# A squared-ReLU feed-forward kernel: loading all x tiles first on two queues, transposing them in one block, and moving the small loads off GpSimd

## Chip, cores, metric

One core of one Trainium2 chip. The metric is the device time of one execution in microseconds (us). The profiled execution is one of those timed, except for the kernel before, where a further one of 291.46 us was profiled. "Span" is the profiled length from first to last instruction, about 1.7 to 2.1 us shorter than the device time.

## The reference

```python
B, S, D, F = 1, 2048, 576, 4608          # all bf16
def reference(x, w1, b1, w2, b2):
    h = jnp.einsum("bsd,df->bsf", x, w1) + b1
    r = jnp.where(h > 0, h, 0)
    h = r * r
    return jnp.einsum("bsf,fd->bsd", h, w2) + b2
```

## The kernel before

The sequence is cut into four blocks of 512 rows. D = 576 is four chunks of 128 rows and one half chunk of 64. The kernel treats 4 of the 36 column tiles of w1 (`w1n`, four 128-row chunks, and `w1n8`, the last 64 rows) apart from the rest (`w_h`). For the first block, x arrives as four row tiles, TensorE transposes them, VectorE and ScalarE copy the result out of PSUM, and the first four column tiles are computed from it chunk by chunk. That is the start-up stage, about the first 10 us, and it is nearly all that the change touches. After it come the half-row matmuls on `w_h` (PSUM tile `ph`) and the rest. The profile leaves numbers out of names: its `w_h` is `w1_h` in the code, `b_rows` is `b1_rows`, `x_sb` is `xs`, and `w1n` stands for both `w1n` and `w1n8`.

```python
    WARM = [512] * 6 + [128]
    for i, n in enumerate(WARM):                       # warm-up matmuls on a constant
        keep(nc.tensor.matmul(wps[:, 0:n], lhsT=ones[:, 0:P], rhs=ones[:, 0:n], start=True, stop=True))
    # ...
    load_x(nc.sync, 0)                                 # first loads: six from sync, two from ScalarE
    load_x(nc.scalar, 1)
    load_w1n(nc.sync, 0)
    load_x(nc.scalar, 2)
    load_w1n(nc.sync, 1)
    load_x(nc.sync, 3)
    for k in range(2, NK):                             # NK = 4
        load_w1n(nc.sync, k)
    # ... identity for the transposes on GpSimd
    nc.gpsimd.memset(b1_rows[:], 0.0)
    nc.gpsimd.dma_start(out=b1_rows[0:NFT, :], in_=b1.rearrange("(ft p) -> ft p", p=P))
    # ...
                # first block ("k_outer"): part(h, k) is 4 matmuls of 256 columns,
                # half h of the rows, chunk k
                for j in range(2):
                    for k in range(NK):
                        x_transpose(j, k)
                for j in range(2):
                    x_transpose(j, NK)
                x_copies(0)                            # chunks 0, 2: VectorE; 1, 3: ScalarE
                part(0, 0)
                for k in range(NK + 1):
                    x_transpose(2, k)
                part(0, 1)
                part(0, 2)
                for k in range(NK + 1):
                    x_transpose(3, k)
                x_copies(1)
                dup_windows(0)
                part(0, 3)
                part(1, 0)
                make_b1T()                             # transposes the bias rows, needed by the evictions
                for k in range(1, NK):
                    part(1, k)
    # ... then the half-row pairs on w1n8, then a_rows(0) on w_h
```

## Time and profile before

| | before |
|---|---|
| device time, 6 runs | 291.0 us median (290.65 to 291.53) |
| span of the profiled run | 289.6 us |
| PE busy | 285.5 us, 99% |
| first half-row `w_h` matmul | 10.29 us |

The page names the engine that bounds the kernel (part 1) and follows the chain of work that ended last (part 4). Columns of part 1: busy us, share of the span, number of instructions.

```profile
PE 285.5 (99%) x2027; PEld 139.9 (48%) x2032; DVE 78.6 (27%) x176; ACT 96.7 (33%) x154; POOL 2.3 (1%) x10
...
PE 98%; DMA 1%; issue 0%; DVE 0%
```

There is hardly idle time to win. The chain, read for the first microseconds alone, shows what can be moved (columns: start us, us, what):

```profile
...
0.73 2.99 DMA x_sb<-in_x_dram
3.73 0.04 issue
3.77 1.25 PE tb L149 x10
5.02 0.86 PE pn L227 x4
5.88 0.53 PE tb L149 x5
6.42 0.98 PE pn L227 x8
7.40 0.28 PE tb L149 x5
7.68 0.87 PE pn L227 x8
8.55 0.06 PE b1T_ps L166
8.61 1.31 PE pn L227 x12
...
```

After the first x tile there is no entry but PE, save 0.04 us of issue. The same work does not always cost the same: five transposes take 0.53 us at 5.88 and 0.28 us at 7.40. The array runs at half rate first and at full rate from about 6.5 us on. The page's row of granted clock does not show this (it has 9 in every slice), so it is read from the spacing of matmul starts: 107 then 56 ns for a transpose, 213 then 109 ns for 256 columns. The kept trace also holds a record of the granted clock; its full rate begins at 6.51 us here.

The busy time by stretches of the stage (columns: stretch, its length, then busy us and count for PE, weight loads, VectorE, ScalarE, GpSimd, then clock, DMA share, GB/s):

```profile
5.40:6.40 1.00, 1.00 (x9) 0.83 (x8) 0.15 (x1) 0.00 (x0) 0.18 (x1) 1.00 0.99 277
6.40:7.40 1.00, 1.00 (x12) 0.89 (x10) 0.00 (x0) 0.00 (x0) 0.00 (x0) 1.00 0.97 217
7.40:8.40 1.00, 1.00 (x14) 0.91 (x12) 0.80 (x4) 0.65 (x2) 0.00 (x0) 1.00 0.56 128
8.40:9.40 1.00, 1.00 (x12) 0.91 (x10) 0.97 (x2) 0.00 (x0) 0.00 (x0) 1.00 0.75 171
```

PE is busy in all of each. The bias rows, loaded from GpSimd, landed at 5.45 us and were wanted at 8.39: nobody waited for them.

### The profile page before, as it was taken

What the parts mean: (1) busy time and instruction counts of PE and PEld (TensorE: products, weight loads), DVE (VectorE), ACT (ScalarE), POOL (GpSimd) and SP (SyncE); (2) the same over time, 40 slices, a digit from 0 to 9 for tenths busy, and PEclk for the clock granted to TensorE, in tenths of its full rate; (3) what the DMA queues carried; (4) which work ended last, traced back from release to release, by engine and by line L of the source; (5) the groups of instructions that cost most, each with busy time, mean ns of one, the idle gap of its engine ahead of it and who ended that gap; (6) DMA issues with size and microseconds to landing.
All of it is one profiled execution on the core that took longest, in us unless ns stands there. A gap on an engine that the chain in (4) does not pass through costs nothing.

```text
span 289.6 us, 4693 instructions
## 1 busy us (share of the span) xinstructions
PE 285.5 (99%) x2027; PEld 139.9 (48%) x2032; DVE 78.6 (27%) x176; ACT 96.7 (33%) x154; POOL 2.3 (1%) x10
## 2 busy tenths in 40 slices
PE   8999999999999999999999999999999999999996
PEld 5544444444444555555544444444444455555555
DVE  1644554444500200000015444444440001100001
ACT  2566666666500000000027666666670000000000
POOL 3000000000000000000000000000000000000000
PEclk9999999999999999999999999999999999999999
DMA  7999999400001200000000000000000110000000
GB/s 198 221 245 188 308 389 212 92 0 2 0 14 25 52 16 18 16 16 18 16 16 2 1 2 0 2 0 2 0 2 0 36 38 16 16 16 19 33 16 18
DMA packets 31605, 16.52 MB, mean 57 GB/s; under 512 B 15700, under 2 KB 31584, under 8 KB 31584
## 3 DMA queue, kind: packets, MB, share of 16 engines
q1 hardware_dynamic: 31232, 15.91, 22.3%
q10 hardware_dynamic: 288, 0.30, 0.4%
q8 instruction: 16, 0.26, 0.4%
q14 instruction: 5, 0.04, 0.0%
q0 software_dynamic: 64, 0.01, 0.0%
HBM read 11.36 MB, written 2.36 MB: 47 GB/s over the span
## 4 chain that ended last, share of the span: by engine, by line
PE 98%; DMA 1%; issue 0%; DVE 0%
PE ph L188 42%; PE po L289 38%; PE pt L270 11%; PE pn L209 4%; PE pn L227 1%; DMA x_sb<-in_x_dram 1%; PE tb L149 1%; PE ph L190 1%; PE pn L203 1%; DVE o_sb L291 0%; PE b1T_ps L166 0%; PE pn L205 0%
## 5 line engine op out<-in xcount | busy, mean ns | idle before, releaser
L190 PE MATMUL ph<-xTw,w_h 64*128 64x512 bf16 x576 | 124.6, 376 | 0.0
L188 PE MATMUL ph<-xTw,w_h 64*128 64x512 bf16 x576 | 124.6, 376 | 0.0
L289 PE MATMUL po<-w_sb,hT 128*128 128x448 bf16 (+2 forms) x612 | 109.4, 341 | 0.0
L176 ACT ACTIVATE r<-ph,b1T 128x512 bf16<-128x512 f32 x128 | 81.1, 685 | 41.6 <-PE ph L190 41.6
L188 PEld LDWEIGHTS <-w_h 64*128 64x128 bf16 x576 | 54.1, 94 | 68.3
L289 PEld LDWEIGHTS <-hT 128*128 128x128 bf16 x612 | 58.5, 98 | 51.0
L177 DVE TENSOR_TENSOR hT<-r 128x512 bf16<-128x512 bf16 x144 | 61.2, 426 | 75.9 <-ACT r L176 75.5
L190 PEld LDWEIGHTS <-w_h 64*128 64x128 bf16 x576 | 54.1, 94 | 0.0
L291 DVE TENSOR_TENSOR o_sb<-po,b_bc 128x448 bf16<-128x448 f32 (+2 forms) x17 | 10.2, 597 | 125.8 <-PE po L289 125.8
L270 PE MATMUL pt<-hT,w_sb 128*128 128x512 bf16 x142 | 31.3, 379 | 0.1
L176 ACT ACTIVATE r<-pn,b1T 128x512 bf16<-128x512 f32 x16 | 10.3, 688 | 61.0 <-PE pn L205 59.6
L270 PEld LDWEIGHTS <-w_sb 128*128 128x128 bf16 x144 | 14.1, 98 | 17.0
L273 ACT ACTIVATE oT<-pt,b2T 128x512 bf16<-128x512 f32 x4 | 2.8, 688 | 28.3 <-PE pt L270 28.3
L209 PE MATMUL pn<-xTw,w1n 128*128 128x512 bf16 x45 | 10.4, 379 | 0.4 <-issue 0.3
L209 PEld LDWEIGHTS <-w1n 128*128 128x128 bf16 x48 | 4.5, 98 | 6.0 <-issue 0.8
L227 PE MATMUL pn<-xTw,w1n 128*128 128x256 bf16 x32 | 4.6, 295 | 0.0
L63 PE MATMUL wps<-const-bfloat16-1.0 128*128 128x512 bf16 (+1 forms) x7 | 2.8, 582 | 0.8 <-PEq L344 0.8
L227 PEld LDWEIGHTS <-w1n 128*128 128x128 bf16 x32 | 3.3, 107 | 0.5
L156 DVE COPY xTw<-tb 128x256 bf16<-128x256 bf16 x4 | 1.1, 292 | 6.7 <-PE tb L149 6.7
L119 DVE COPY xTw<-xTw 64x2048 bf16<-64x2048 bf16 x4 | 2.8, 690 | 0.2
L120 DVE COPY xTw<-xTw 64x2048 bf16<-64x2048 bf16 x4 | 2.7, 687 | 0.1
L149 PE MATMUL tb<-ident,x_sb 128*128 128x128 bf16 x20 | 2.4, 288 | 0.2 <-DMA x_sb<-in_x_dram 0.2
(23 smaller groups left out, 15.2 us busy)
## 6 DMA issues: line engine op xcount, KB each, us to landing
w_sb<-in_w_dram SPq DMA_DIRECT2D x4, 1296.0 KB, 12.7
w_h<-in_w_dram SPq DMA_DIRECT2D x14, 288.0 KB, 6.2
out_dram<-o_sb SPq DMA_DIRECT2D x15, 112.0 KB, 1.7
w_h<-in_w_dram SPq DMA_DIRECT2D x4, 144.0 KB, 3.5
w1n<-in_w_dram SPq DMA_DIRECT2D x4, 128.0 KB, 3.9
out_dram<-ot SPq DMA_DIRECT2D x4, 128.0 KB, 2.0
x_sb<-in_x_dram ACTq DMA_DIRECT2D x2, 144.0 KB, 2.9
x_sb<-in_x_dram SPq DMA_DIRECT2D x2, 144.0 KB, 3.4
```

Source lines behind the costliest of these rows:

```text
L63: keep(nc.tensor.matmul(wps[:, 0:n], lhsT=ones[:, 0:P], rhs=ones[:, 0:n], start=True, stop=True))
L149: keep(nc.tensor.transpose(bank[:, slot, qc], xs[:, j, c0:c0 + P], ident[:]))
L176: keep(nc.scalar.activation(out=r[:], in_=bank[:], func=ACT.Relu, bias=b1T[:, ft:ft + 1], scale=1.0))
L177: keep(nc.vector.tensor_tensor(out=hTs[sb][:, ft, :], in0=r[:], in1=r[:], op=ALU.mult))
L188: keep(nc.tensor.matmul(bx[:], lhsT=w1_h[0:H, LO_C[i], jc], rhs=xT[0:H, LO_W[i], :], start=(i == 0), stop=(i == NC - 1)))
L190: keep(nc.tensor.matmul(by[:], lhsT=w1_h[H:P, UP_C[i], jc], rhs=xT[H:P, UP_W[i], :], start=(i == 0), stop=(i == NC - 1)))
L203: keep(nc.tensor.matmul(banks[2 * i][:], lhsT=w1n8[0:H, i, :], rhs=xT[0:H, SPC, :], start=start, stop=stop, skip_group_check=order == "k_o ...
L209: keep(nc.tensor.matmul(banks[g][:], lhsT=w1n[:, k, g * P:(g + 1) * P], rhs=xT[:, O + k, :], start=start, stop=stop))
L227: keep(nc.tensor.matmul(banks[g][:, hc], lhsT=w1n[:, k, g * P:(g + 1) * P], rhs=xT[:, O + k, hc], start=(h == 0 and k == 0), stop=False, s ...
L270: keep(nc.tensor.matmul(pt[:], lhsT=w2_sb[:, ft, DM:D], rhs=hT[:, ft, :], start=(i == 0), stop=(i == NFT - 1)))
L289: keep(nc.tensor.matmul(po[:, 0:d1 - d0], lhsT=hT[:, ft, jj * P:(jj + 1) * P], rhs=w2_sb[:, ft, d0:d1], start=(i == 0), stop=(i == NFT - 1)))
L291: keep(nc.vector.tensor_tensor(out=o_sb[:, d0:d1], in0=po[:, 0:d1 - d0], in1=b2_bc[:, d0:d1], op=ALU.add))
```

## The change

Intent: let all x tiles arrive first, on two queues, and then the w1 chunks; transpose all of x before the first matmul; bring the last 64 rows of w1 in pieces of 1 KB instead of 256 bytes (each of the two loads then brings 64 KB instead of 32); take the loads off GpSimd; bring w2 in two loads instead of four. The number of TensorE instructions stays (the counts below differ by a few records that are missing from the traces). The core of the diff:

```diff
-    WARM = [512] * 6 + [128]
+    WARM = [512] * 6 + [256]
...
+    b1_rows = const.tile([P, P], BF16, name="b1_rows")
+    nc.vector.memset(b1_rows[:], 0.0)
     load_x(nc.sync, 0)
     load_x(nc.scalar, 1)
-    load_w1n(nc.sync, 0)
-    load_x(nc.scalar, 2)
-    load_w1n(nc.sync, 1)
-    load_x(nc.sync, 3)
-    for k in range(2, NK):
-        load_w1n(nc.sync, k)
+    load_x(nc.sync, 2)
+    load_x(nc.scalar, 3)
+    for k in range(NK):
+        load_w1n(nc.sync if k % 2 == 0 else nc.scalar, k, k + 1)
...
-    nc.gpsimd.memset(b1_rows[:], 0.0)
-    nc.gpsimd.dma_start(out=b1_rows[0:NFT, :], in_=b1.rearrange("(ft p) -> ft p", p=P))
...
     keep(nc.scalar.activation(out=warm[:], ...))      # its table load took 1.28 us
+    for h in range(2):
+        load_w1n8(nc.scalar, h)
+    keep(nc.scalar.dma_start(out=b1_rows[0:NFT, :], in_=b1.rearrange("(ft p) -> ft p", p=P)))
...
     def x_copies(h):
-        # chunks 0, 2 on VectorE; 1, 3 on ScalarE, one instruction each
+        for k in (0, 1):
+            keep(nc.vector.tensor_copy(out=xT0[:, O + k, hc], in_=tb[h][0][:, k, :]))
+        keep(nc.scalar.copy(out=xT0[:, O + 2:O + 4, hc], in_=tb[h][1][:, 0:2, :]))
...
                 for j in range(2):
-                    for k in range(NK):
-                        x_transpose(j, k)
-                # ... interleaved with part(0, 0) to part(0, 2)
+                    x_transpose(j)
                 x_copies(0)
+                for j in range(2, RT):
+                    x_transpose(j)
                 x_copies(1)
                 dup_windows(0)
-                part(0, 3)
+                for k in range(NK):
+                    part(0, k)
                 part(1, 0)
                 make_b1T()
                 for k in range(1, NK):
```

Left out: the PSUM pools of the transposes, the layout of `w1n8`, w2 in two loads, and the b2 column on the sync queue.

More of the change, by code (lines that the diff above doesn't have):

```diff
@@ L57 @@
     ps_o = ctx.enter_context(tc.tile_pool(name="ps_o", bufs=4, space=PSUM))
-    wps = ps_o.tile([P, 512], FP32, name="wps", tag="po")
+    wps = ps_h.tile([P, 512], FP32, name="wps", tag="ph")
     ones = nc.const_aps.tensor(1.0, [P, 512], BF16)
-    WARM = [512] * 6 + [128]
+    WARM = [512] * 6 + [256]
     for i, n in enumerate(WARM):
@@ L66 @@
     w1n = wpool.tile([P, NK, GW], BF16, name="w1n")
-    w1n8 = wpool.tile([P, G // 2, P], BF16, name="w1n8")
+    w1n8 = wpool.tile([P, GW], BF16, name="w1n8")
     w1_h = wpool.tile([P, NC, FH], BF16, name="w1_h")
@@ L72, in load_x, with load_w1n @@
         keep(eng.dma_start(out=xs[:, rt, :], in_=x2[rt * P:(rt + 1) * P, :]))
-    def load_w1n(eng, k):
-        keep(eng.dma_start(out=w1n[:, k, :], in_=w1[k * P:(k + 1) * P, 0:GW]))
+    def load_w1n(eng, k0, k1):
+        src = w1[k0 * P:k1 * P, 0:GW].rearrange("(k p) f -> p k f", p=P)
+        keep(eng.dma_start(out=w1n[:, k0:k1, :], in_=src))
     def load_w1n8(eng, h):
-        src = w1[NK * P:D, 0:GW].rearrange("p (i h f) -> p i h f", h=2, f=P)
-        keep(eng.dma_start(out=w1n8[h * H:(h + 1) * H, :, :], in_=src[:, :, h, :]))
+        keep(eng.dma_start(out=w1n8[h * H:(h + 1) * H, :], in_=w1[NK * P:D, 0:GW]))
     def load_w1(eng, h, j0, j1):
@@ L83, in load_w1 @@
                       in_=w1_v[:, :, GW + h * FH + j0 * P:GW + h * FH + j1 * P]))
+    b1_rows = const.tile([P, P], BF16, name="b1_rows")
+    nc.vector.memset(b1_rows[:], 0.0)
     load_x(nc.sync, 0)
     load_x(nc.scalar, 1)
-    load_w1n(nc.sync, 0)
-    load_x(nc.scalar, 2)
-    load_w1n(nc.sync, 1)
-    load_x(nc.sync, 3)
-    for k in range(2, NK):
-        load_w1n(nc.sync, k)
+    load_x(nc.sync, 2)
+    load_x(nc.scalar, 3)
+    for k in range(NK):
+        load_w1n(nc.sync if k % 2 == 0 else nc.scalar, k, k + 1)
     ident = const.tile([P, P], BF16, name="ident")
     make_identity(nc, ident[:])
-    b1_rows = const.tile([P, P], BF16, name="b1_rows")
-    nc.gpsimd.memset(b1_rows[:], 0.0)
-    nc.gpsimd.dma_start(out=b1_rows[0:NFT, :], in_=b1.rearrange("(ft p) -> ft p", p=P))
-    b2_col = const.tile([P, 1], BF16, name="b2_col")
-    nc.gpsimd.dma_start(out=b2_col[:], in_=b2[DM:D].rearrange("(d o) -> d o", o=1))
-    b2T = const.tile([P, 1], FP32, name="b2T")
-    nc.gpsimd.tensor_copy(out=b2T[:], in_=b2_col[:])
     warm = const.tile([P, 1], FP32, name="warm")
     keep(nc.scalar.activation(out=warm[:], in_=nc.const_aps.tensor(0.0, [P, 1], FP32), func=ACT.Relu))
+    for h in range(2):
+        load_w1n8(nc.scalar, h)
+    keep(nc.scalar.dma_start(out=b1_rows[0:NFT, :], in_=b1.rearrange("(ft p) -> ft p", p=P)))
     E3, O, SPC, E = 0, 1, 5, 6
@@ L130 @@
     w2_view = w2.rearrange("(ft p) d -> p ft d", p=P)
-    W2CH = 9
+    W2CH = 18
     def load_w2(c):
@@ L140, with x_transpose @@
     HS = SB // 2
-    tb_po = [ps_o.tile([P, 2, HS], BF16, name="tb", tag="po") for _ in range(2)]
-    tb_ph = [ps_h.tile([P, 2, HS], BF16, name="tb", tag="ph") for _ in range(4)]
-    half_banks = [tb_ph, None]
-    def x_transpose(j, k):
+    tb = [[ps_h.tile([P, 4, HS], BF16, name="tb", tag="ph") for _ in range(2)] for _ in range(2)]
+    PLACE = [(0, 0), (0, 1), (1, 0), (1, 1), (0, 2)]
+    T_ORDER = [0, 1, NK, 2, 3]
+    def x_transpose(j):
         h, q = divmod(j, 2)
-        qc = slice(q * P, (q + 1) * P)
-        bank, slot, c0 = (half_banks[h][k], 0, k * P) if k < NK else (half_banks[h][2], 1, D - P)
-        keep(nc.tensor.transpose(bank[:, slot, qc], xs[:, j, c0:c0 + P], ident[:]))
+        for k in T_ORDER:
+            bank, slot = PLACE[k]
+            c0 = k * P if k < NK else D - P
+            keep(nc.tensor.transpose(tb[h][bank][:, slot, q * P:(q + 1) * P], xs[:, j, c0:c0 + P], ident[:]))
     def x_copies(h):
         hc = slice(h * HS, (h + 1) * HS)
-        for k in range(NK):
-            src = half_banks[h][k][:, 0, :]
-            if k % 2 == 0:
-                keep(nc.vector.tensor_copy(out=xT0[:, O + k, hc], in_=src))
-            else:
-                keep(nc.scalar.copy(out=xT0[:, O + k, hc], in_=src))
-        keep(nc.vector.tensor_copy(out=xT0[:, E3, hc], in_=half_banks[h][2][:, 1, :]))
+        for k in (0, 1):
+            keep(nc.vector.tensor_copy(out=xT0[:, O + k, hc], in_=tb[h][0][:, k, :]))
+        keep(nc.scalar.copy(out=xT0[:, O + 2:O + 4, hc], in_=tb[h][1][:, 0:2, :]))
+        keep(nc.vector.tensor_copy(out=xT0[:, E3, hc], in_=tb[h][0][:, 2, :]))
     b1T = const.tile([P, NFT], FP32, name="b1T")
     def make_b1T():
-        b1T_ps = ps_o.tile([P, P], BF16, name="b1T_ps", tag="po")
+        b1T_ps = ps_h.tile([P, P], BF16, name="b1T_ps", tag="ph")
         keep(nc.tensor.transpose(b1T_ps[:], b1_rows[:], ident[:]))
@@ L198, in a_full @@
         for g in range(G):
-            pool, tag = (ps_o, "po") if g < 2 else (ps_h, "ph")
+            pool, tag = (ps_o, "po") if g < 2 or order == "k_outer" else (ps_h, "ph")
             banks.append(pool.tile([P, SB], FP32, name="pn", tag=tag))
         def pair(i, start, stop):
-            keep(nc.tensor.matmul(banks[2 * i][:], lhsT=w1n8[0:H, i, :], rhs=xT[0:H, SPC, :],
+            keep(nc.tensor.matmul(banks[2 * i][:], lhsT=w1n8[0:H, 2 * i * P:(2 * i + 1) * P], rhs=xT[0:H, SPC, :],
                              start=start, stop=stop, skip_group_check=order == "k_outer"))
-            keep(nc.tensor.matmul(banks[2 * i + 1][:], lhsT=w1n8[H:P, i, :], rhs=xT[H:P, E3, :],
+            keep(nc.tensor.matmul(banks[2 * i + 1][:], lhsT=w1n8[H:P, (2 * i + 1) * P:(2 * i + 2) * P], rhs=xT[H:P, E3, :],
                              start=start, stop=stop, skip_group_check=order == "k_outer"))
@@ L220, in a_full @@
             if order == "k_outer":
-                tb_new = [ps_h.tile([P, 2, HS], BF16, name="tb", tag="ph") for _ in range(2)]
-                half_banks[1] = tb_new + tb_po
                 def part(h, k):
@@ L231, in a_full @@
                 for j in range(2):
-                    for k in range(NK):
-                        x_transpose(j, k)
-                for j in range(2):
-                    x_transpose(j, NK)
+                    x_transpose(j)
                 x_copies(0)
-                part(0, 0)
-                for k in range(NK + 1):
-                    x_transpose(2, k)
-                part(0, 1)
-                part(0, 2)
-                for k in range(NK + 1):
-                    x_transpose(3, k)
+                for j in range(2, RT):
+                    x_transpose(j)
                 x_copies(1)
                 dup_windows(0)
-                part(0, 3)
+                for k in range(NK):
+                    part(0, k)
                 part(1, 0)
@@ L296 @@
         load_w1(nc.sync, 1, j0, j1)
-        if j0 == 0:
-            load_w1n8(nc.sync, 0)
-            load_w1n8(nc.sync, 1)
     load_xT(1)
@@ L303 @@
         load_w1(nc.sync, 1, j0, j1)
+    b2_col = const.tile([P, 1], BF16, name="b2_col")
+    keep(nc.sync.dma_start(out=b2_col[:], in_=b2[DM:D].rearrange("(d o) -> d o", o=1)))
+    b2T = const.tile([P, 1], FP32, name="b2T")
+    nc.gpsimd.tensor_copy(out=b2T[:], in_=b2_col[:])
     keep(nc.sync.dma_start(out=b2_bc[:], in_=b2.partition_broadcast(P)))
-    for c in (0, 2, 1, 3):
+    for c in range(2):
         load_w2(c)
```

## The prediction

> **What bounds it now.** TensorE. The page gives PE 285.5 us busy of a 289.6 us span (99%), and the chain that ended last is 98% PE. What is not PE on that chain is the first x tile's load (2.99 us, 1%) and the last eviction and store (286.9 us to the end). The waits of PE sum to 1.3 us. Everything the change touches, except the second half of the w2 loads, lies in the first 10.3 us, before the first half-row matmul of w1 (10.29 us in the timeline); w2 lands by 47.9 us and is first read at 76 us, so its two larger chunks, like the moved b2 loads, cost and gain nothing.
>
> **What PE does in those 10.3 us.** Warm-up from 0.78, then 20 transposes, 32 matmuls of 256 columns, the bias transpose and four half-row matmuls, from 3.77 us (first x tile landed at 3.73) with hardly a hole. I find two: 0.06 us before the first 256-column matmul, and 0.10 us before the half-row pairs (9.75 to 9.85), just after the second window copy on VectorE ended at 9.72. The rest of the lost time is the array's rate: starts are 107 ns apart for a transpose and 213 ns for 256 columns until about 6.5 us, then 56 and 109 ns. [...]
>
> **What the change does.** The instruction order shows the same number of TensorE instructions; only their order in this stage differs. All 20 transposes come first (20 x 107 = 2.14 us, to 5.91), then 32 matmuls, about 2.5 of them at half rate (estimate, if full rate comes again at 6.45): 5.91 + 0.54 + 29.5 x 0.109 + 0.056 = 9.72, half-row matmuls of w1 from about 10.15 instead of 10.29. So it saves the two holes, about 0.15 us. x tile 0 and 1 are first on their queues in both, so the 3.73 us stays. x tiles 2 and 3 should land near 4.2 to 4.6 instead of 4.1 and 6.1; the w1 chunks by about 6.3 instead of 7.05, none of which PE waited for. VectorE's window copies should end near 8.2 instead of 9.72.
>
> New risks: ScalarE now issues four loads (about 0.45 us each), a 1.28 us table load, then three more loads, so its first copy is near 5.5 us and the bias rows land near 7.8 to 8.2, wanted by PE near 8.35: slack of a few tenths. [...]
>
> **Prediction.** 290.6 us; 8 times in 10 between 289.9 and 291.5. The moment of full rate varies between runs (before: 290.65, 290.72, 291.53), more than the gain. Faster by over 2%: 0.005; within 2%: 0.99; slower by over 2%: 0.005.
>
> **What would show it.** Transposes in one block from about 3.77 to 5.9; no PE wait over 0.2 us; the first half-row w1 matmul at 10.0 to 10.3, if full rate comes near 6.4; from there to the end the same 279 us within 0.3.
>
> **What would make it wrong.** A late bias row or w1 chunk that stalls PE; [...] a later first x tile; a late w1 stream starving the half-row stage.

290.72, less the two holes of about 0.15 us, is about 290.6.

## The result, and the profile after

The changed kernel took 291.95 us (median of 6, 291.35 to 292.32) against 291.0 us. Ratios here and below are the mean time of a kernel's fast runs over that of the other kernel's fast runs of the same rounds, so they are not quite the ratio of the medians. This one is 1.0031, 95% interval 1.0016 to 1.0046: a loss of about 0.9 us, small but clear of the noise. The predicted 290.6 and its upper end 291.5 were both too low.

The same views of the changed kernel, parts 1 and 4 of the page first:

```profile
PE 285.9 (99%) x2032; PEld 139.8 (48%) x2032; DVE 78.4 (27%) x177; ACT 96.3 (33%) x152; POOL 0.9 (0%) x7
...
PE 98%; DMA 1%; DVE 0%; issue 0%
```

At this size of difference the averages say nothing. The chain of the first microseconds does:

```profile
...
0.78 2.93 PE wps L63 x7
3.71 1.93 PE tb L146 x18
5.63 3.04 DMA b_rows<-in_b_dram
8.67 0.05 issue
8.72 0.23 PE b1T_ps L159
8.95 1.31 PE pn L217 x12
...
```

The path that decides no longer runs through TensorE's matmuls in the middle of the stage. It runs through the load of the bias rows, issued at 5.63 us and landed at 8.67, and only 12 of the 32 matmuls remain on the chain after it. (The link from the transposes to the issue of this load is an inference of the view; what held the issue is shown below.) The stretches show what that leaves of PE:

```profile
5.40:6.40 1.00, 1.00 (x13) 0.92 (x11) 0.69 (x3) 0.16 (x1) 0.00 (x0) 1.00 0.64 164
6.40:7.40 1.00, 0.78 (x8) 0.56 (x6) 0.05 (x1) 0.92 (x2) 0.00 (x0) 1.00 1.08 252
7.40:8.40 1.00, 0.95 (x9) 0.60 (x7) 0.97 (x2) 0.00 (x0) 0.00 (x0) 1.00 1.00 227
8.40:9.40 1.00, 0.68 (x7) 0.63 (x8) 0.55 (x2) 0.00 (x0) 0.00 (x0) 1.00 0.88 216
```

There are two holes. Busy time hides a part of each, because the last matmul's modelled end runs into it; from start to start the first is 488 ns where 109 is normal (6.39 to 6.88 us), so 0.38 us, and the second 640 ns (8.08 to 8.72), so 0.53 us. Together 0.91 us. That this equals the loss of the medians is in part chance: the two profiles differ by only 0.34 us at the end of the stage, as the one of before was of one of its longer runs (291.46 us), with a late full rate. What the holes cost on average, the experiments have to show. The timeline names what ended them (columns: start, us, engine, line, operation, tiles, count, idle before and releaser):

```profile
3.93 0.20 ACT L97 ACTIVATE warm<-const-float32-0.0 128x1 f32<-128x1 f32 x1
4.12 0.49 ACTq L79 DMA_DIRECT2D w1n<-in_w_dram  x1
...
5.63 0.57 ACTq L100 DMA_DIRECT2D b_rows<-in_b_dram  x1
...
6.24 1.07 ACT L152 COPY xTw<-tb 128x512 bf16<-128x512 bf16 x2 [2.11 <-DVE xTw L151]
6.88 1.47 PE L217 MATMUL pn<-xTw,w1n 128*128 128x256 bf16 x12 [0.22 <-ACT xTw L152]
...
8.72 0.23 PE L159 MATMUL b1T_ps<-ident,b_rows 128*128 128x128 bf16 x1 [0.37 <-DMA b_rows<-in_b_dram]
```

ScalarE finished issuing the second small w1 load at 4.61 us. Its next instruction, the load of the bias rows, started at 5.63, a whole microsecond later, and the copy that stands behind it at 6.24, though its data (the transposes of x tiles 0 and 1) were in PSUM by 4.77. PE's first hole ends with that copy, the second with the bias rows. The releaser printed for the copy, VectorE, is the event that came last among its semaphores, not the reason: the queue itself was held.

What held it is a wait just ahead of the issue, which ended at 5.57 us. The view of this source line has it as an instruction of its own (count, duration in ns, first and last start in us):

```profile
L100 ACTq EVENT_SEMAPHORE  x1: 17/17/17, 5.6 to 5.6; - x1
L100 ACTq DMA_DIRECT2D b_rows<-in_b_dram x1: 567/567/567, 5.6 to 5.6; - x1
```

The trace names a completion semaphore for each of these loads and records sixteen updates of it as the load lands (for w1 chunk 1 from 4.80 to 5.55 us). The first eight loads have eight different ones (numbers 100 and 103 to 109), and the later loads take these eight again, on the sync and ScalarE queues together. The bias rows are the load that comes round to the semaphore of w1 chunk 1, which was still in flight, and they wait for it: its sixteenth update came at 5.55 us, 0.02 us before the wait ended. The two small w1 loads were held in the same way, for less: they went out at 3.44 and 4.12 us, each 0.02 us after the landing of the x tile whose semaphore they reuse (3.42 and 4.10). In the kernel before, ScalarE issued two loads, and none waited for a semaphore.

Everything later is the same. From the first half-row matmul to the last matmul of the program it is 276.37 us in before (10.29 to 286.66), in after (10.63 to 287.00), and in every profile. So each profile is described by the start of that stage alone: device time less stage start is 281.0 to 281.3 us in all fifteen.

### The profile page after: what moved, and what is told of

Same layout as the page of the kernel before. It is cut to its first block, busy times and chain, and to the rows that moved or that the text cites. A ratio compares the mean times of both kernels' runs of the same rounds, so it can differ in the third digit from the quotient of the medians.

```text
span 289.9 us, 4695 instructions
## 1 busy us (share of the span) xinstructions
PE 285.9 (99%) x2032; PEld 139.8 (48%) x2032; DVE 78.4 (27%) x177; ACT 96.3 (33%) x152; POOL 0.9 (0%) x7
## 4 chain that ended last, share of the span: by engine, by line
PE 98%; DMA 1%; DVE 0%; issue 0%
PE ph L181 42%; PE po L272 38%; PE pt L253 11%; PE pn L202 4%; DMA b_rows<-in_b_dram 1%; PE wps L63 1%; PE tb L146 1%; PE ph L183 1%; PE pn L196 1%; PE pn L217 0%; DVE o_sb L274 0%; PE b1T_ps L159 0%; PE pn L198 0%
## 5 line engine op out<-in xcount | busy, mean ns | idle before, releaser
L217 PE MATMUL pn<-xTw,w1n 128*128 128x256 bf16 x32 | 4.0, 272 | 0.2 <-ACT xTw L152 0.2
L196 PE MATMUL pn<-xTw,w1n 64*128 64x512 bf16 x8 | 2.4, 379 | 0.0
L198 PE MATMUL pn<-xTw,w1n 64*128 64x512 bf16 x8 | 2.4, 379 | 0.0
```

The costliest lines, as they stand in the source:

```text
L196: keep(nc.tensor.matmul(banks[2 * i][:], lhsT=w1n8[0:H, 2 * i * P:(2 * i + 1) * P], rhs=xT[0:H, SPC, :], start=start, stop=stop, skip_grou ...
L217: keep(nc.tensor.matmul(banks[g][:, hc], lhsT=w1n[:, k, g * P:(g + 1) * P], rhs=xT[:, O + k, hc], start=(h == 0 and k == 0), stop=False, s ...
```

## The experiments

The theories:

- **A**: the loss is the two holes, both made on ScalarE's queue.
- **B**: the block of transposes delays the array's full rate.
- **C**: the loss lies outside the start-up stage.
- **D** and **E** came later, for what was left.

Each kernel was timed in rounds with the kernel before on the same chip. All results were correct. "Stage start" is the first half-row `w_h` matmul of the profile; "full rate" is where the spacing of starts halves, as far as waits let it be seen; the clock records, kept in all traces but those of the changed kernel and w0_first, agree with it within 0.1 us.

| kernel | median us | ratio to before (95%) | full rate, us | PE holes, us | stage start, us |
|---|---|---|---|---|---|
| changed | 291.95 | 1.0031 (1.0016 to 1.0046) | 5.5 | 0.38 + 0.53 | 10.63 |
| b1_late | 291.33 | 1.0020 (1.0007 to 1.0033) | 3.6 | 0.12 + 0.69 + 0.58 | 10.14 |
| copies_dve | 291.75 | 1.0029 (1.0017 to 1.0042) | 4.7 | 0.90 + 0.53 + 0.22 | 11.02 |
| late_dve | 291.21 | 1.0011 (0.9997 to 1.0024) | 6.4 | none | 10.06 |
| gps_b1 | 291.04 | 1.0008 (0.9995 to 1.0020) | 3.5 | 0.18 + 1.10 | 10.01 |
| before_again | 290.91, one run, state unknown | | 5.7 | 0.06 | 9.84 |
| two_queue | 291.97 | 1.0037 (1.0024 to 1.0050) | 4.5 | 0.22 + 0.61 + 1.05 | 11.09 |
| cold_before | 292.06 | 1.0043 (1.0030 to 1.0056) | 6.8 | 0.06 | 10.27 |
| cold_gps | 292.09 | 1.0039 (1.0026 to 1.0052) | 6.8 | 0.06 | 10.26 |
| b1_mid | 291.37 | 1.0012 (1.0000 to 1.0024) | 6.7 | none | 10.25 |
| w0_first | 291.86 | 1.0043 (1.0016 to 1.0071) | by 5.3 | 0.69 | 9.94 |
| reorder | 291.06 | 1.0001 (0.9986 to 1.0016) | 3.9 | 0.27 + 0.35 + 0.14 + 0.28 | 10.06 |
| gps_oneq | 291.02 | 1.0001 (0.9987 to 1.0014) | 4.2 | 0.16 + 0.45 + 0.31 | 10.13 |
| after_again | 291.66 | 1.0025 (1.0012 to 1.0037) | 5.2 | 0.48 + 0.76 | 10.76 |

A fixed hole of 0.10 us before the half-row pairs is in all of them and not listed. A profile is of one execution, the ratio of five or six. The difference of two ratios carries the noise of both, about 0.002; a smaller one is not resolved.

### b1_late: the bias transpose moved back

```diff
-                part(1, 0)
-                make_b1T()
-                for k in range(1, NK):
+                for k in range(NK):
                     part(1, k)
+                make_b1T()
```

> The changed kernel with one edit: the bias transpose stands after all 32 matmuls of 256 columns instead of after the 20th. Theory A (the loss is two PE holes from ScalarE's queue: 0.38 us waiting for its first copy, 0.53 us waiting for the bias rows): the 0.53 us hole goes, the 0.38 us hole stays, first half-row w1 matmul near 10.1 us if full rate comes near 5.5, time about 0.5 us under the changed kernel: 291.3 to 291.6. Rival B (the transposes in one block delay the full array rate, holes are hidden elsewhere) and rival C (the loss lies outside the first 11 us): no change, 291.8 to 292.1.

Measured: 291.33 us, ratio 1.0020, about 0.3 us less than the changed kernel (0.0011 of 291), which is inside the noise: these runs do not show how much the bias rows' wait alone cost. The wait for the bias rows is gone from its waits; the wait for ScalarE's copy is not. In this profile full rate came at 3.6 us, and PE, earlier at the w1 chunks, waited 0.69 us for chunk 0, which landed at 5.42, a third hole that theory A had not named. The views of waits (columns: engine, tile and line, releaser, total us, times, longest) show both, and here the profile gives the true reason for ScalarE's late copy: the landing of the w1 chunk whose semaphore the bias rows needed.

```profile
ACT xTw L152 <- DMA w1n<-in_w_dram: 2.2, 1, 2.2
...
PE pn L217 <- DMA w1n<-in_w_dram: 0.5, 1, 0.5
...
PE pn L217 <- ACT xTw L152: 0.4, 1, 0.4
```

### copies_dve: the copies of chunks 2 and 3 on VectorE

```diff
-        keep(nc.scalar.copy(out=xT0[:, O + 2:O + 4, hc], in_=tb[h][1][:, 0:2, :]))
+        keep(nc.vector.tensor_copy(out=xT0[:, O + 2:O + 4, hc], in_=tb[h][1][:, 0:2, :]))
```

> The changed kernel with one edit: VectorE instead of ScalarE makes the copies of chunks 2 and 3. Theory A: the 0.38 us hole goes, but the bias rows still land near 8.6 us, so the wait for them grows by as much; first half-row w1 matmul stays at 10.6, time within 0.2 us of the changed kernel. If the two holes add independently: 0.4 us faster. Rivals B and C: no change either, but then without a hole of about 0.9 us before the bias transpose.

Measured: 1.0029, within noise of the changed kernel's 1.0031. No gain, as A expects: with the copy out of the way PE only reaches the wait for the bias rows sooner. The two holes are in series ahead of one landing, they do not add: in the profiles of the changed kernel, copies_dve and after_again the bias rows landed at 8.67, 9.06 and 8.80 us, and the stage start followed 1.96 us later in each. The profile does not show the single wait of 0.9 us that was expected: in it w1 chunk 0 landed at 6.07 us and chunk 2 at 7.53 (5.35 and 6.00 in the changed kernel's profile), PE waited 0.90 and 0.53 us for those, and only 0.22 us were left to wait for the bias rows.

### late_dve: the edits of b1_late and copies_dve together

> Both edits: bias transpose after all 32 matmuls, chunk 2 and 3 copies on VectorE. Theory A: no PE hole over 0.15 us in the first 11 us, first half-row w1 matmul at 9.6 to 10.1 depending on when full rate comes, time 0.8 to 1.0 us under the changed kernel: about 291.0, level with the kernel before or 0.1 to 0.2 us under it. Rivals B and C: 291.8 to 292.1.

Measured: 291.21 us, 1.0011. PE has no hole but the fixed 0.10 us. Of the 0.9 us lost (0.0031), about 0.6 us (0.0020) come back. That is at the edge of the noise, but the five runs (291.00 to 291.33) also lie below all five of copies_dve (291.38 to 292.05), which was timed on the same chip in the same rounds. Theories B and C, which expected no change, are out as the main cause.

### gps_b1: the bias rows from GpSimd again

```diff
-    nc.vector.memset(b1_rows[:], 0.0)
...
     make_identity(nc, ident[:])
+    nc.gpsimd.memset(b1_rows[:], 0.0)
+    nc.gpsimd.dma_start(out=b1_rows[0:NFT, :], in_=b1.rearrange("(ft p) -> ft p", p=P))
...
-    keep(nc.scalar.dma_start(out=b1_rows[0:NFT, :], in_=b1.rearrange("(ft p) -> ft p", p=P)))
```

> The changed kernel with the bias rows loaded from GpSimd again, as in the kernel before (clear and load). Theory A: bias rows land near 5.5 us, ScalarE's first copy starts near 4.9 us instead of 6.24, both holes go, time about 291.0, like late_dve. If the wait for a reused completion semaphore is not what held ScalarE: copy still after 6 us. Rivals B and C: 291.8 to 292.1.

Measured: 291.04 us, 1.0008; about 0.7 us of the 0.9 come back (0.0023), and these five runs too (290.92 to 291.33) lie below all of copies_dve. The bias rows landed at 5.43 and ScalarE's copy started at 4.73 instead of 6.24. So the one edit that takes this load off ScalarE's queue removes both holes:

```profile
4.22 0.47 ACTq L79 DMA_DIRECT2D w1n<-in_w_dram  x1
4.73 1.07 ACT L152 COPY xTw<-tb 128x512 bf16<-128x512 bf16 x2 [0.60 <-PE tb L146]
```

Its profile shows another, however (timeline, PE):

```profile
5.92 2.36 PE L217 MATMUL pn<-xTw,w1n 128*128 128x256 bf16 x20 [0.94 <-DMA w1n<-in_w_dram]
```

In this run full rate was there before the first transpose, PE was through with the transposes at 4.8 us and had nothing to do until chunk 0 of w1 landed at 5.87. In the kernel before chunk 0 landed at 4.32, because it stood ahead of two of the x tiles. That became theory D: with all x first, an early full rate is of no use.

### before_again, cold_before, cold_gps: the moment of full rate

before_again is the kernel before with a comment changed. cold_before is the kernel before, cold_gps is gps_b1, each without warm-up matmuls:

```diff
-    WARM = [512] * 6 + [128]          # [512] * 6 + [256] in gps_b1
+    WARM = []
```

> The kernel before with only a comment changed, for a second profile of it. All runs so far have 276.37 us from the first half-row w1 matmul to the last matmul, so only the start of that stage differs. Theory D (full rate comes at a phase that changes from run to run, and the profile of before showed a late one, about 6.45 us): full rate at another moment of 3.0 to 6.5 us; if it is early, the first half-row w1 matmul at 9.5 to 9.9 us instead of 10.29, with PE waiting for x tile 3 and the last w1 chunks (landing 6.1 to 7.05). If the 10.29 us were a fixed property of before: 10.2 to 10.4 again.

> The kernel before without its seven warm-up matmuls[...]. Theory D: PE is bound by its own half rate, no wait for a w1 chunk; first half-row w1 matmul near 11 to 12 us, time 1 to 2 us over before.

> gps_b1 (changed kernel, bias rows from GpSimd) without its warm-up matmuls. Theory D: at half rate the transposes last until about 5.7, so the wait for w1 chunk 0 (5.4 to 6.1) shrinks to under 0.4 us and the loss against the kernel before goes: equal to cold_before within 0.2 us, or up to 0.3 us faster (the first x tile landed 0.25 us earlier in all x-first profiles). If the block of transposes delays full rate: cold_gps slower than cold_before by 0.5 us or more, with full rate later by 1 us or more.

Measured: before_again reached full rate at 5.7 us instead of 6.5 and the stage start at 9.84 us instead of 10.29, with the first x tile landing 0.16 us earlier too. So the profile that the prediction was built on was a late one, and 10.29 is no property of the kernel. Over the warmed profiles full rate came between 3.5 and 6.7 us.

The expected waits for x tile 3 and the last chunks did not show in before_again: full rate at 5.7 was probably not early enough for them. The cold kernels lost 1.1 to 1.3 us, as expected for before, and came out level: 1.0043 and 1.0039. (The stage start of 11 to 12 us expected for cold_before rested on an estimate; measured was 10.27.) The wait of gps_b1 for chunk 0 is gone (0.06 us left). That agrees with D, but what it should remove is only 0.0008, which these intervals do not resolve. Against B they are clear. With 20 transposes in a block as the first 2.1 us of PE's work, full rate still came at 6.75 us by the clock record, 3.28 us after the first transpose, and in cold_before 3.24 us after its first:

```profile
3.47 2.31 PE L146 MATMUL tb<-ident,x_sb 128*128 128x128 bf16 x20 [3.47 <-DMA x_sb<-in_x_dram]
5.64 2.01 PE L217 MATMUL pn<-xTw,w1n 128*128 128x256 bf16 x12
```

In these two profiles the block of transposes does not delay it.

### two_queue: the kernel before, with its first loads issued from both queues

```diff
     load_w1n(nc.sync, 1)
-    load_x(nc.sync, 3)
-    for k in range(2, NK):
-        load_w1n(nc.sync, k)
+    load_x(nc.scalar, 3)
+    load_w1n(nc.scalar, 2)
+    load_w1n(nc.sync, 3)
```

> The kernel before with one edit: x tile 3 and w1 chunk 2 are issued from ScalarE's queue, so the eight first loads are out by 2.6 us instead of 3.5; small loads, order of transposes and matmuls as before. Theory D: w1 chunk 0 lands near 4.3 as before, the last chunk near 6.2 to 6.8 instead of 7.05, first half-row w1 matmul 0.2 to 0.6 us earlier when full rate comes early and unchanged when late: mean 0.1 to 0.4 us under before. If the loads do not bound before at all: 290.9, no change.

Measured: 291.97 us, 1.0037: slower by 1.1 us, where 0.1 to 0.4 us of gain was expected. The last of these loads was issued at 2.15 us instead of 3.12, but chunk 1 landed at 6.05 us (5.67 in before_again), x tile 3 at 6.48 (5.89), chunk 2 at 7.54 (6.23) and chunk 3 at 7.33 (6.90). PE waited for two of them:

```profile
6.09 0.61 PE L227 MATMUL pn<-xTw,w1n 128*128 128x256 bf16 x4 [0.45 <-DMA w1n<-in_w_dram]
7.58 0.61 PE L227 MATMUL pn<-xTw,w1n 128*128 128x256 bf16 x4 [0.88 <-DMA w1n<-in_w_dram]
```

The rate did not rise with the second queue. The stretch from 2 to 7 us, in before_again first and in two_queue second (the last two columns are the DMA engines' busy share and GB/s):

```profile
2.00:7.00 5.00, 4.99 (x36) 3.46 (x35) 0.78 (x3) 1.78 (x4) 0.88 (x3) 1.00 0.95 282
```

```profile
2.00:7.00 5.00, 4.20 (x28) 2.54 (x26) 0.78 (x3) 2.13 (x4) 0.88 (x3) 1.00 0.98 279
```

The engines were full in both (0.95 and 0.98) and the rate the same (282 and 279 GB/s): what the second queue saved was issue time (2.15 instead of 3.12 us). Packets of both queues moved side by side (from 2.1 to 2.4 us in two_queue 48 of the sync queue's and 32 of ScalarE's), and transfers of the two queues land in pairs (chunks 2 and 3 here at 7.54 and 7.33, in gps_b1 chunks 0 and 1 at 5.87 and 6.05). So what is wanted first can share the rate with what is wanted later, such as the `w_h` loads that the sync queue starts at 3.46 us. That it did so here, and that this made two_queue slower, is argued, not shown. Each of these loads updates its semaphore sixteen times as its parts land, and a late load is late through a few of them: of chunk 3, 13 parts were in by 5.83 us and the other three at 6.35, 6.91 and 7.33. In copies_dve, which has the loads of the changed kernel unaltered, 14 parts of chunk 1 were in by 5.12 us and the last at 6.55 (5.55 in the changed kernel). So a load can land later with nothing changed in its order. Why a few parts lag, and more in some runs than in others, stays open.

### b1_mid: the bias rows ahead of the small w1 loads, on the same queue

```diff
+    keep(nc.scalar.dma_start(out=b1_rows[0:NFT, :], in_=b1.rearrange("(ft p) -> ft p", p=P)))
     for h in range(2):
         load_w1n8(nc.scalar, h)
-    keep(nc.scalar.dma_start(out=b1_rows[0:NFT, :], in_=b1.rearrange("(ft p) -> ft p", p=P)))
```

> The changed kernel with one edit: on ScalarE's queue the bias rows are loaded before the two small w1 loads instead of after them. Theory A2 (a load whose completion semaphore is still owed to an earlier load blocks everything behind it on that queue; there are eight, in turn): the bias rows now reuse an early x tile's semaphore, issue near 4.1 and land near 7, so the wait for them goes; the second small w1 load now reuses that of w1 chunk 1 and is held until that chunk lands (5.4 to 6.1), so ScalarE's copy still starts after 6 us and PE still waits for it or for w1 chunk 2. Time as b1_late: about 0.5 us under the changed kernel, 291.2 to 291.5. If the bias load itself, not the semaphore, held the copy: copy at about 5.2 and both holes gone, about 291.0.

Measured: 291.37 us, 1.0012, 0.55 us better than the changed kernel (0.0019, just at the noise). As expected of A2 (the semaphore holds the queue, not the bias load itself) the bias rows went out at 3.49, landed at 6.84, and nobody waited for them. The hold moved to the load that now comes round to chunk 1's semaphore, the second small w1 load: it was issued at 5.70 us, just after that chunk landed at 5.68, and ScalarE's copy still started at 6.22.

```profile
3.49 0.56 ACTq L98 DMA_DIRECT2D b_rows<-in_b_dram  x1
3.92 0.20 ACT L97 ACTIVATE warm<-const-float32-0.0 128x1 f32<-128x1 f32 x1
4.41 1.76 ACTq L79 DMA_DIRECT2D w1n<-in_w_dram  x2
6.22 0.59 ACT L152 COPY xTw<-tb 128x512 bf16<-128x512 bf16 x1 [2.10 <-PE tb L146]
```

The same number of loads, the same queue, another load in the place that waits: the hold belongs to the semaphore's turn, not to the bias load. In this profile full rate came late (6.7 us), and so PE did not feel the late copy.

### w0_first and reorder: two attempts to win with theory D

w0_first is gps_b1 with chunk 0 of w1 issued ahead of x tile 2 on the sync queue; ScalarE's order stays:

```diff
     load_x(nc.sync, 0)
     load_x(nc.scalar, 1)
-    load_x(nc.sync, 2)
+    load_w1n(nc.sync, 0, 1)
     load_x(nc.scalar, 3)
-    for k in range(NK):
-        load_w1n(nc.sync if k % 2 == 0 else nc.scalar, k, k + 1)
+    load_x(nc.sync, 2)
+    load_w1n(nc.scalar, 1, 2)
+    load_w1n(nc.sync, 2, 3)
+    load_w1n(nc.scalar, 3, 4)
```

reorder is the kernel before with another order of work on TensorE:

```diff
                 part(0, 1)
-                part(0, 2)
                 for k in range(NK + 1):
                     x_transpose(3, k)
                 x_copies(1)
                 dup_windows(0)
-                part(0, 3)
+                part(0, 2)
                 part(1, 0)
+                part(1, 1)
+                part(0, 3)
                 make_b1T()
-                for k in range(1, NK):
+                for k in range(2, NK):
                     part(1, k)
```

> gps_b1 with one edit: w1 chunk 0 is issued ahead of x tile 2 on the sync queue. Theory D (what is left of the loss is w1 chunk 0 landing at 5.4 to 6.1 behind all x tiles): chunk 0 lands near 4.3, x tile 2 near 5; the 1.1 us wait before the first 256-column matmul shrinks to about 0.5 us or moves to x tile 2; first half-row w1 matmul 9.8 to 10.1; time 0 to 0.2 us under gps_b1, which the interval will hardly resolve. If chunk 0 is not what it is about: no shorter wait.

> The kernel before with one edit: x tile 3 is transposed right after w1 chunk 1's first-half matmuls, and chunks 0 and 1 of the second half run before chunk 3 of the first, so that less PE work hangs on the chunk that lands last (7 us). Loads as before. Theory D: with early full rate no wait for chunk 3, first half-row w1 matmul 0.1 to 0.3 us earlier; with late full rate equal or up to 0.15 us later (wait for the second half's copy). Time 0.1 us under before, within 0.2 either way.

Measured: w0_first, 291.86 us, 1.0043 with the widest spread of all (291.07 to 293.55). Its profile is of its fastest run and looks as expected: chunk 0 landed at 4.18, the wait moved to x tile 2 and was 0.69 us, stage start 9.94. But two of its six runs took 293.5 us and were not profiled. What cost 2 us in them stays open. The expectation of a gain failed. reorder is level with before, 1.0001; its profile, with full rate at 3.9 us, started the next stage at 10.06. PE waited 0.35 us for chunk 1 there, 0.14 for x tile 3 and 0.28 for chunk 2: with an early full rate the loads of the kernel before make PE wait as well. It is no improvement. No kernel beat the kernel before.

### gps_oneq and after_again: is the rest the split over two queues?

gps_oneq is gps_b1 with all w1 loads on the sync queue, in order:

```diff
-        load_w1n(nc.sync if k % 2 == 0 else nc.scalar, k, k + 1)
+        load_w1n(nc.sync, k, k + 1)
...
-    for h in range(2):
-        load_w1n8(nc.scalar, h)
...                                                    # after the first pair of w_h loads
+            load_w1n8(nc.sync, 0)
+            load_w1n8(nc.sync, 1)
```

> gps_b1 (changed kernel, bias rows from GpSimd) with all w1 loads, the small ones too, issued from the sync queue in order; ScalarE's queue keeps x tiles 1 and 3 alone. Theory E (w1 chunks split over two queues land together and sometimes a microsecond late; from one queue they land in order, as in the kernel before): chunk 0 lands near 4.9 to 5.3, the last near 6.7 to 7.1, the spread of the times shrinks; time at or under gps_b1: ratio to before 0.999 to 1.001. If it stays at 1.001 or above, the rest of the loss is not due to the split.

> The changed kernel with only a comment changed, beside gps_oneq on one chip and for a second profile at another phase of the array's rate. Theory A: the first half-row w1 matmul stands about 1.96 us after the bias rows' landing (bias landing 8.4 to 8.9, matmul 10.3 to 10.8) unless full rate comes after about 6.3 us; time 1.002 to 1.0045 of before.

Measured on one chip: gps_oneq 291.02 us, 1.0001; the changed kernel 291.66 us, 1.0025, its loss seen a second time. Its second profile shows the same picture: bias rows issued at 5.53 and wanted at 8.09, PE holes of 0.48 and 0.76 us, stage start 10.76, which is the expected 1.96 us after the landing of the bias rows (8.80). The runs of the two do not overlap (290.86 to 291.27 and 291.58 to 291.93): this pair shows the loss, and its removal, most clearly.

So a kernel with all x tiles first, the block of transposes and the 1-KB pieces, but with its bias rows from GpSimd and its w1 loads in order on one queue, is level with the kernel before. Chunk 0 landed at 5.62, later than the expected 5.3 at most, the last at 7.30, in order; times spread over 0.41 us as gps_b1's had. The step from gps_b1 (1.0008) to gps_oneq (1.0001) is 0.2 us, inside both intervals: the split over two queues came with a loss in two_queue, and may be the rest here, if there is a rest.

## Why the prediction was wrong

- **What bounds the kernel, and where the change acts: right.** All of the difference is in the first 11 us; the rest is 276.37 us in every profile. w2 in two loads and the b2 loads moved nothing, as that constant stretch shows. The class, within 2%, was right.
- **The step that failed: "ScalarE now issues four loads [...], then three more loads, so its first copy is near 5.5 us and the bias rows land near 7.8 to 8.2, wanted by PE near 8.35: slack of a few tenths."** The sum of issue times left out a wait. The seventh load on this queue had to wait until 5.57 us for w1 chunk 1, whose completion semaphore it reuses, and everything behind it on the queue waited too. The bias rows landed at 8.67 and were wanted at 8.19 (PE had full rate earlier than assumed), so PE stood for 0.53 us; the copy started at 6.24 instead of 5.5, and PE stood for 0.38 us. Taking the load off the queue (gps_b1) gave back about 0.7 of the 0.9 us; moving it within the queue (b1_mid) moved the hold to its neighbour. A late bias row was named as the first risk, but priced at no cost.
- **"the w1 chunks by about 6.3 instead of 7.05, none of which PE waited for": right for the last chunk, silent on the first.** The last landed at 6.17, but chunk 0, the one wanted first, went from 4.32 to 5.35. When full rate comes early PE does wait for it: 0.69 us in b1_late, 1.10 us in gps_b1. Landing the last chunk earlier is no gain if the first lands later.
- **"it saves the two holes, about 0.15 us": wrong in its larger part.** The 0.10 us before the half-row pairs was put down to VectorE's window copy, which had ended just before. In the changed kernel that copy ended at 8.76 us, 1.4 us before the pairs, and the hole is there at the same 96 ns. It is there again at about 150 us, where 128-row matmuls of 512 columns give way to such pairs (312 ns from start to start where 216 is normal), in all fifteen profiles. So it goes with the change from 128-row to 64-row matmuls (95 to 97 ns ahead of the pairs in every profile); why was not shown. The view of waits had called it "issue", not a wait for VectorE.
- **The risk that the block of transposes postpones full rate: it did not come true.** In the changed kernel full rate came at 5.5 us, right at the end of the block, and in after_again at 5.2, within it.
- **The range was too narrow on the side that mattered.** It was set around three runs of before with a median of 290.72; six gave 291.0. The baseline explains 0.3 us of the miss of 1.35; the missed holes, 0.6 to 0.7 us by the experiments, and the gain of 0.15 us that did not come explain most of the rest. The gain was worked out on a profile of a 291.46 us run but taken off a median of 290.72.

## What to carry to other kernels

Count a load's waits, not only its issue time: where loads take completion semaphores in turn, as eight were taken here, a load in the middle of an engine's queue can wait for an unrelated large transfer (the 9 KB of bias rows for the 128 KB of w1 chunk 1, until 5.57 us), and it holds the engine's compute instructions behind it (the copy, with data ready at 4.77 us, started at 6.24). Keep small late loads off the queue of an engine whose next copy feeds TensorE (gps_b1: about 0.7 us back). A second queue did not add bandwidth here, where the DMA engines were already full (279 GB/s against 282); one queue with the loads in the order in which they are wanted was not slower in either of the two pairs compared. When a start-up stage is judged from one trace, find out first how much the moment of full rate varies; here it lay anywhere in about 3 us over the warmed profiles (3.5 to 6.7 us; 0.8 us apart in two profiles of the kernel before), more than the effect that was sought.
